# One maximum step of 11 units takes two key blocks in one, and attention's output is turned by DMA

## The chip, the cores and the metric

The kernel runs on one core of one Trainium2 chip. TensorE multiplies matrices into PSUM; VectorE, ScalarE and GpSimd (POOL in the profile) work on tiles; SP only issues DMAs and waits. The metric is the device time of one launch in microseconds. A time of the profile is that of one profiled execution.

## The reference

A transformer layer over 2048 rows of width 512, in bf16: layer norm, attention with 32 heads of width 16, a residual, layer norm, a gated feed-forward of width 1792, a residual.

```python
def _A_ref(x, wqkv, wo):
    B, S, D = x.shape
    H = 32
    Dh = D // H
    qkv = (lambda x, *d: x.transpose(*d))((x @ wqkv).reshape(B, S, 3, H, Dh), 2, 0, 3, 1, 4)
    q, k, v = qkv[0], qkv[1], qkv[2]
    scores = jnp.einsum("bhqd,bhkd->bhqk", q, k) * (Dh ** -0.5)
    p = _softmax(scores, axis=-1)
    o = jnp.einsum("bhqk,bhkd->bhqd", p, v)
    return (lambda x, *d: x.transpose(*d))(o, 0, 2, 1, 3).reshape(B, S, D) @ wo
...
h = x + _A_ref(_layernorm(x, axis=-1), A_wqkv, A_wo)
h2 = h + (_gelu(n @ w_gate) * (n @ w_up)) @ w_down        # n = _layernorm(h)
```

## The kernel before

**Units and ticks.** Attention is cut into 64 units: 8 groups of 256 query rows (`gi`), and in each 8 slots of four heads. A unit has 16 ticks. In each tick a *maximum pass* (`p1_pair`, `p1_consume`) has TensorE write two banks of scores, 128 queries x 512 keys for each of two heads (L797), and VectorE reduce both in one `tensor_reduce` of 1024 columns to two maxima in `PM` (L806). Tick j of a unit takes key block `j // 4`, query half `(j // 2) % 2`, and two of the four heads. GpSimd folds the four key blocks' maxima into the row maximum in steps (`negm_part` after ticks 8 and 12, L817 to L824; `negm_pre` after tick 15, L832 to L840), splits it into three bf16 terms, and SP turns them by a DMA transpose (`negm_post`, L846); four ticks later GpSimd adds the turned rows to the queries (L851), whose spare rows meet ones in the keys. So the scores come out of TensorE with their maximum subtracted.

**The second pass** follows 24 ticks behind (`P2_START`): in each tick TensorE computes two tiles of transposed scores of the earlier unit (`p2_tile`, L867: two matmuls of 256 columns into one bank), and ScalarE takes their exponentials (`p2_consume`, L896: 512 columns each). Banks 0 to 3 hold the maximum pass's two pairs; banks 4 to 7 are shared by the exponentials' tiles and one *dense* item at a time.

**The dense stream** (`Dense`) is everything else that TensorE does, cut into items that run a piece per tick: the products of the probabilities with the values (`item_pv`, L910, once in each unit), the turn of the output (`item_ofin`, L936), the output projection (`item_oproj`, L1015), and the feed-forward's gates, ups (L1089) and downs (L1139) of the group before. `prio` holds items with a due tick, `ready` the rest in order. A gate or an up starts only if the program's own count of ScalarE's backlog, `act_lag`, is at most `LAG_START`. Filler matmuls (L1299) take up what TensorE has left. `defer(k, fn)` runs a step k ticks later. `PoolStream` hands GpSimd its operations within a budget of 1.19 us a tick.

**Turn of the output.** After `item_pv`, ScalarE copies the 256 columns of a slot to `OA` (fp32). In every second unit `item_ofin` turns two slots with four fp32 matmuls against an identity, ScalarE copies the result to `OAT`, and GpSimd takes the inverse of the sums (a power, L945, 16 columns) and multiplies (L949) into `Otok`. When all eight slots of a group are there, `post_onT` turns `Otok` by DMA, and projection, residual, layer norm, `post_hnT` (a DMA transpose again) and the feed-forward of that group follow.

**Feed-forward.** A gate's item makes ScalarE copy the product to `g_sb`; GpSimd computes the polynomial (L1079, L1080, L1081), ScalarE the tanh (L1072), GpSimd two more steps (L1077, L1078) and, with the up's copy, the product (L1131). Seven pairs of gate and up and two downs make a group.

**The order of the work** on each engine is the order in which the program's loop over ticks emits it. Each engine runs its list in order, and each instruction waits for the semaphores of what it depends on. SP's list holds all DMAs.

**The tail.** After the last maximum, 24 ticks of exponentials are left, then the last group's projection, layer norm (its inverse root on GpSimd, L1262) and feed-forward (`tail_a`, `tail_b`); what of the dense stream is left then is run there.

Of the kernel before, what the change touches and what calls it, by code (L numbers as in the profile page):

```python
# [222 lines left out]
ADDX = 4  # L223
# [5 lines left out]
LAG_START = 0.4  # L229
LAG_OP = 0.2  # L230
TANH_LAG = 2


def bass_sequential_preLN__mha_block__geglu_ffn__prompt_kernel(nc, A_x, A_wqkv, A_wo, B_x, B_w_gate, B_w_up, B_w_down, out):
    dbg = None
    with ExitStack() as es:
# [74 lines left out]
        OAT = at("OAT", [128, 2, 272], FP32)  # L311
# [189 lines left out]
        def startable(it, room):  # L501
            if it[0] is item_gate and par_busy[it[1][1] % 2] and room < 10:
                return False
            if it[0] is item_down and it[1] == (GL - 1, 1) and not force[0]:
                return False
            if it[0] is item_down and it[1][1] == 0 and not force[0]:
                return not gut_left.get(it[1][0], 0) and dense.now >= gut_last.get(it[1][0], 0) + 1
            return it[0] is not item_projT or not (qks_busy.get(("a", qk_n[0] % 4)) or qks_busy.get(("b", qk_n[0] % 2)))

        class Dense:  # L510
            def __init__(self):
                self.prio = []
                self.ready = []
                self.gen = None
# [13 lines left out]
            def _start(self, item):  # L528
                genfn, a, est, nb = item
                if self.single:  # L530
# [5 lines left out]
            def piece(self):  # L536
                if self.single and self.pause > 0:
                    return 0
                while True:
                    if self.gen is None:  # L540
# [4 lines left out]
                        if self.prio and (not self.single or self.prio[0][3] <= self.now):  # L545
                            self._start(self.prio.pop(0))
                        elif self.ready and (not self.single or ((act_lag[0] <= LAG_START or force[0] or self.ready[0][0] not in (item_gate, item_up)) and startable(self.ready[0], lim - self.now) and self.ready[0][3] <= self.now and self.now + self.ready[0][2] + PAUSE - 1 <= lim)):
# [25 lines left out]
        dense = Dense()  # L573

# [19 lines left out]
        class PoolStream:  # L594

            def __init__(self):
                self.q = []
                self.budget = 0.0
            def add(self, ops, then=None):
# [4 lines left out]
            def spend(self, cost):  # L604
                self.budget -= cost
            def run(self, flush=False):
                while self.q and (flush or self.budget >= min(self.q[0][0], 1.0)):
                    if not flush and self.q[0][0] > 2.0 and dense.now % 16 in (1, 2, 3, 13, 14, 15):
                        break
                    cost, fn, then = self.q.pop(0)  # L610
                    self.budget -= cost
                    fn()
# [190 lines left out]
        def p1_consume(ui, tiles):  # L803
            par = ui % 2
            (b, qt, kc, g), (b2, _, _, g2) = tiles
            P.op("dve", lambda e: e.tensor_reduce(out=PM[:, par, qt, kc, g:g + 2], in_=pbank[:, b:b + 2, :], axis=AX.X, op=ALU.max),  # L806
                 reads=[("pb", b), ("pb", b2)], writes=[("PM", par, qt, kc, g), ("PM", par, qt, kc, g2)])

        def negm_part(ui, k):
# [10 lines left out]
            else:  # L820
# [3 lines left out]
                P.op("pool", lambda e: e.tensor_scalar(out=m3, in0=m3, scalar1=-1.0, scalar2=None, op0=ALU.mult), reads=[("MXm", par)], writes=[("MXm", par)])  # L824

# [16 lines left out]
        def negm_post(ui):  # L842
# [6 lines left out]
            def add():  # L849
                pool.spend(0.7)  # L850
                P.op("pool", lambda e: e.tensor_tensor(out=q_ap, in0=q_ap, in1=STG[:, par, :], op=ALU.add), reads=[("STG", par), ("qT", slot, c, hf)], writes=[("qT", slot, c, hf)])  # L851
                q_ready.add(ui)
            defer(ADDX, add)
# [45 lines left out]
        def item_pv(b, ui):  # L899
# [18 lines left out]
            evac_act(OA[:, par, 256 * col:256 * col + 256], pbank[:, b, 0:256], [("pb", b)], [("OA", par, col)], cost=0.41)  # L918
            if gi == GL and slot >= NSLOT - 2:
                if col == 0:  # L920
                    dense.add(item_ofin, gi, (slot,), front=True, est=3, not_before=dense.now + 3)
            elif col == 1:
                dense.add(item_ofin, gi, (slot - 1, slot), front=True, est=3, not_before=dense.now + 3)
# [6 lines left out]
        oat_busy = {}  # L930
        def item_ofin(b, gi, slots):
            gp, par, ns = gi % 2, slots[0] // 2 % 2, len(slots)
            assert not oat_busy.get(par), "GpSimd too far behind"
            for q in range(2):
                for sp in range(ns):
# [487 lines left out]
```

## Time and profile before

| | |
|---|---|
| median of 3 runs | 1243.8 us (1243.76 to 1245.08) |
| profiled execution | 1243.51 us |
| its span, first to last instruction | 1241.8 us |
| mean granted TensorE clock | 1.00 |
| VectorE busy | 1188.9 us, 1087 instructions |
| ScalarE busy | 1199.5 us, 2444 instructions |
| GpSimd busy | 764.4 us, 1540 instructions |

In the rows, `out<-in` names what an instruction writes and reads, then come partitions x elements and the type, `xcount`, the busy time in us, the mean duration in ns, and behind the second bar the idle time of the engine just before these instructions with what ended most of it. The durations of successive instructions of one engine overlap: the time that one more instruction costs is the distance from start to start, or a stretch's length over its count, not its duration. The chain of work that ended last is followed back from the last instruction to what released it. A row of a stretch has its bounds in us, its length, then the busy time and the count for PE, PEld, DVE, ACT and POOL (or for those that have any), the clock, the DMA engines' share and GB/s.

### The profile page before, as it was taken

The numbers are of one execution on the slowest core, as the hardware profiler recorded it, in microseconds if no ns is written. First come the engines' busy times: TensorE is split into PE (matmuls) and PEld (weight loads), VectorE is DVE, ScalarE is ACT, GpSimd is POOL, SyncE is SP. The second block draws the span as 40 slices with busy tenths as digits, with TensorE's granted clock in tenths as the row PEclk, the third lists the DMA queues.
The fourth block names the chain that finished last, engine by engine and source line by source line (L and its number), as shares of the span: only waits on it lengthen the run. The fifth ranks groups of instructions, "written<-read, shape, count | busy, mean of one in ns | idle before, by whom it ended". The sixth has DMA issues, their size and how long they took to land.

```text
span 1241.8 us, 31457 instructions
## 1 busy us (share of the span) xinstructions
PE 1137.1 (92%) x12700; PEld 438.6 (35%) x12700; DVE 1188.9 (96%) x1087; ACT 1199.5 (97%) x2444; POOL 764.4 (62%) x1540
## 2 busy tenths in 40 slices
PE   8999888899999999999999998999999999999989
PEld 3333222233333333333333333333333333333335
DVE  8999999999999999999999999999999999999933
ACT  7899999999999999999999999999999999999992
POOL 8557774467746765476645777367654767547760
PEclk9999999999999999999999999999999999999999
DMA  5101004300010000100010000100002000100000
GB/s 151 31 22 28 24 19 125 93 5 4 6 31 12 6 6 6 38 5 6 4 27 18 3 6 6 27 17 6 6 4 36 10 4 6 27 19 3 6 12 18
DMA packets 50800, 27.45 MB, mean 22 GB/s; under 512 B 36064, under 2 KB 49632, under 8 KB 50656
## 3 DMA queue, kind: packets, MB, share of 16 engines
q1 hardware_dynamic: 50656, 25.45, 8.3%
q8 instruction: 101, 1.65, 0.6%
q14 instruction: 43, 0.35, 0.1%
HBM read 11.80 MB, written 2.10 MB: 11 GB/s over the span
## 4 chain that ended last, share of the span: by engine, by line
DVE 60%; ACT 27%; PE 10%; POOL 2%; issue 1%; DMA 1%; POOLq 0%
DVE PM L806 60%; ACT PTM L896 14%; ACT PTG L896 4%; ACT PTE L896 3%; PE pbank L1139 2%; PE pbank L797 1%; PE pbank L867 1%; PE pbank L1089 1%; ACT th_sb L1072 1%; PE pbank L739 1%; ACT g_sb L641 1%; ACT OnT L1029 1%; PE pbank L427 1%; PE pbank L676 1%; DMA STG<-ST 1%
## 5 line engine op out<-in xcount | busy, mean ns | idle before, releaser
L806 DVE TENSOR_REDUCE PM<-pbank 128x2 f32<-128x1024 f32 x1024 | 1162.5, 1213 | 5.9 <-PE pbank L867 3.3
L896 ACT ACTIVATE PTM<-pbank 128x512 bf16<-128x512 f32 x1357 | 721.0, 668 | 4.7
L867 PE MATMUL pbank<-QT,KT 32*128 32x256 bf16 x4096 | 495.2, 273 | 12.2 <-ACT PTM L896 5.1
L797 PE MATMUL pbank<-KT,QT 32*128 32x512 bf16 x2048 | 394.2, 382 | 46.4 <-DVE PM L806 23.8
L1299 PE MATMUL pbank<-ones_bf,ident 128*128 128x512 bf16 x814 | 250.8, 384 | 27.3 <-ACT PTM L896 2.4
L797 PEld LDWEIGHTS pbank<-KT,QT 32*128 32x128 bf16 x2048 | 104.4, 91 | 392.5 <-DVE PM L806 170.3
L896 ACT ACTIVATE PTG<-pbank 128x512 bf16<-128x512 f32 x407 | 221.4, 660 | 0.8
L867 PEld LDWEIGHTS pbank<-QT,KT 32*128 32x128 bf16 x4096 | 163.6, 92 | 66.2 <-ACT PTM L896 34.7
L896 ACT ACTIVATE PTE<-pbank 128x512 bf16<-128x512 f32 x236 | 135.5, 668 | 0.8
L910 PE MATMUL pbank<-PTM,VA 128*17 128x256 bf16 x2776 | 125.7, 274 | 2.8 <-ACT PTM L884 0.9
L832 POOL TENSOR_TENSOR MX<-PM,MX 128x8 f32<-128x8 f32 x64 | 12.9, 202 | 163.6 <-DVE PM L806 163.6
L1299 PEld LDWEIGHTS pbank<-ones_bf,ident 128*128 128x128 bf16 x814 | 49.4, 97 | 132.5 <-ACT PTM L896 82.7
L945 POOL TENSOR_TENSOR LINV<-OAT,negone 128x16 f32<-128x16 f32 (+1 forms) x32 | 92.7, 2896 | 0.0
L910 PEld LDWEIGHTS pbank<-PTM,VA 128*17 128x17 bf16 x2776 | 59.8, 89 | 47.2 <-issue 29.8
L821 POOL TENSOR_TENSOR MX<-PM,MX 128x8 f32<-128x8 f32 x64 | 13.0, 203 | 101.6 <-DVE PM L806 101.5
L1089 PE MATMUL pbank<-hnT_l,wu_sb 128*128 128x256 bf16 x448 | 66.7, 275 | 3.1 <-ACT PTM L896 0.2
L1089 PE MATMUL pbank<-hnT_l,wg_sb 128*128 128x256 bf16 x448 | 66.9, 275 | 2.4
L1078 POOL TENSOR_TENSOR th_sb<-th_sb,g_sb 128x512 f32<-128x512 f32 x49 | 62.2, 1269 | 4.1
L1081 POOL TENSOR_TENSOR th_sb<-th_sb,g_sb 128x512 f32<-128x512 f32 x49 | 62.1, 1268 | 3.1
L1131 POOL TENSOR_TENSOR GUT<-th_sb,u_sb 128x512 bf16<-128x512 f32 x49 | 62.3, 1271 | 2.0
L1079 POOL TENSOR_TENSOR th_sb<-g_sb 128x512 f32<-128x512 f32 x49 | 51.0, 1041 | 19.2 <-ACT g_sb L641 19.2
L1139 PE MATMUL pbank<-wd_sb,GUT 128*128 128x512 bf16 x224 | 60.2, 382 | 0.6 <-ACT PTM L896 0.2
(154 smaller groups left out, 1100.0 us busy)
## 6 DMA issues: line engine op xcount, KB each, us to landing
QKS<-QKS SPq DMA_DIRECT2D x27, 112.0 KB, 2.2
x_sb<-in_A_x_dram SPq DMA_DIRECT2D x4, 512.0 KB, 5.7
xres<-in_A_x_dram SPq DMA_DIRECT2D x16, 128.0 KB, 2.2
out_dram<-out_sb SPq DMA_DIRECT2D x16, 128.0 KB, 1.9
wg_sb<-in_B_w_gate_dram SPq DMA_DIRECT2D x4, 448.0 KB, 5.2
wu_sb<-in_B_w_up_dram SPq DMA_DIRECT2D x4, 448.0 KB, 6.1
wd_sb<-in_B_w_down_dram SPq DMA_DIRECT2D x3, 512.0 KB, 5.5
STG<-ST SPq DMA_TRANSPOSE x64, 2.3
```

What stands on the lines that cost most here:

```text
L797: P.op("pe", lambda e, g=g, b=b: e.matmul(pbank[:, b, :], QT[32 * g:32 * g + 32, c, slot, 128 * qt:128 * qt + 128], KT[32 * g:32 * g + 32, ...
L806: P.op("dve", lambda e: e.tensor_reduce(out=PM[:, par, qt, kc, g:g + 2], in_=pbank[:, b:b + 2, :], axis=AX.X, op=ALU.max), reads=[("pb", b ...
L867: P.op("pe", lambda e, kt=kt, i=i: e.matmul(pbank[:, b, 256 * i:256 * i + 256], KT[32 * g:32 * g + 32, slot, 128 * kt:128 * kt + 128], QT[ ...
L896: P.op("act", lambda e, b=b, pi=pi: e.activation(out=PTt(pi), in_=pbank[:, b, :], func=ACT.Exp), reads=[("pb", b)], writes=[("PT", pi)], e ...
L910: P.op("pe", lambda e, g=g, kt=kt, pi=pi, i=i: e.matmul(pbank[32 * g:32 * g + 17, b, 0:256], VA[:, kt, 4 * slot + g, :], PTt(pi)[:, 256 * ...
L945: P.op("pool", lambda e: e.tensor_tensor(out=li, in0=oat4[:, :, :, 16], in1=negone[:, 0:8 * ns].rearrange("p (q h) -> p q h", q=2), op=ALU ...
L1078: o(1.27, lambda e: e.tensor_tensor(out=ts_, in0=ts_, in1=gs, op=ALU.mult), [("th", par), ("g", par)])], then=done)
L1081: o(1.27, lambda e: e.tensor_tensor(out=ts_, in0=ts_, in1=gs, op=ALU.mult), [("th", par), ("g", par)])], then=lambda: defer(TANH_LAG, lamb ...
L1089: P.op("pe", lambda e, dc=dc, fc=fc, i=i: e.matmul(pbank[:, b, 256 * i:256 * i + 256], w[:, dc, 128 * fc:128 * fc + 128], hT[:, dc, :], st ...
L1131: P.op("pool", lambda e: e.tensor_tensor(out=o_ap, in0=shp(ts_), in1=shp(us), op=ALU.mult), reads=[("th", par), ("u", par)], writes=o_keys ...
L1139: P.op("pe", lambda e: e.matmul(pbank[:, b, :], GUT[:, fc, 128 * k:128 * k + 128], wd_sb[:, fc, :], start=first, stop=last), reads=[("GUT" ...
L1299: P.op("pe", lambda e: e.matmul(pbank[:, b, :], ident[:], ones_bf[:, 0:512], start=True, stop=True), reads=["ident", "ones_bf"], writes=[( ...
```

## The change

In 11 of the 64 units the maximum over key blocks 2 and 3, for one query half and two heads, is taken in one step. TensorE computes the difference of the two blocks' scores (one matmul with the query, one with its negative `QN`, into one bank), ScalarE writes its positive part to `RB` in fp32, and VectorE adds that to block 2's scores and takes the maximum, max(a + relu(b - a)) = max(a, b), one `tensor_tensor_reduce` for each head. The reduction of block 3 (tick 14 of the unit) is left out: that tick is skipped in the loop, what was deferred moves by one tick, and the two exponential tiles of the skipped tick are taken one each in the next two odd ticks.

```diff
+JOINT = (12, 14, 17, 20, 25, 28, 33, 36, 41, 44, 49)
+J_AT, J_GONE = 10, 14
...
         def p1_consume(ui, tiles):
...
+            if ui in JOINT and (qt, kc, g) == (1, 2, 0):
+                assert y_left[ui] == 0, "differences too late"
+                for b_, g_ in ((b, g), (b2, g2)):
+                    P.op("dve", lambda e, b_=b_, g_=g_: e.tensor_tensor_reduce(out=RB[:, g_, :], in0=pbank[:, b_, :], in1=RB[:, g_, :], scale=1.0, scalar=-3.0e38, op0=ALU.add, op1=ALU.max, accum_out=PM[:, par, qt, kc, g_:g_ + 1]),
+                         reads=[("pb", b_), ("RB", g_)], writes=[("PM", par, qt, kc, g_), ("RB", g_)])
+                return
...
+        def joint_prep(ui):
+            gi, slot = units[ui]
+            c, qt = gi // 2, 2 * (gi % 2) + 1
+            y_left[ui] = 2
+            pool.add([(0.4, lambda: P.op("pool", lambda e: e.tensor_scalar(out=QN[:], in0=QT[:, c, slot, 128 * qt:128 * qt + 128], scalar1=-1.0, scalar2=None, op0=ALU.mult),
+                                         reads=[("qT", slot, c, gi % 2)], writes=["QN"]))], then=lambda: defer(1, lambda: dense.extra.extend([(item_diff, (ui, g), 2, 0) for g in (0, 1)])))
+
+        def item_diff(b, ui, g):
...
+            P.op("pe", lambda e: e.matmul(pbank[:, b, :], QT[32 * g:32 * g + 32, c, slot, 128 * qt:128 * qt + 128], KT[32 * g:32 * g + 32, slot, 1536:2048], start=True, stop=False, tile_position=(32 * g, 0)),
...
+            P.op("pe", lambda e: e.matmul(pbank[:, b, :], QN[32 * g:32 * g + 32, :], KT[32 * g:32 * g + 32, slot, 1024:1536], start=False, stop=True, tile_position=(32 * g, 0)),
...
+            act_more(0.48)
+            P.op("act", lambda e: e.activation(out=RB[:, g, :], in_=pbank[:, b, :], func=ACT.Relu), reads=[("pb", b)], writes=[("RB", g)], extra_deps=dG)
...
+            if p1_ok and tick // 16 in JOINT and tick % 16 == J_GONE:
+                for i, (k_, fn_) in enumerate(deferred):
+                    deferred[i] = (k_ + 1, fn_)
...
+                behind[0] += 2
+                tick += 1
+                dense.now = tick
+                continue
...
+            more = 1 if behind[0] and tick % 2 else 0
```

The difference's items stand in a third list of the dense stream, `extra`. While a unit of the 11 is at tick 12 or later, or tiles are still behind, `tight()` holds, and no gate, up or tanh starts; a down doesn't start there after tick 8:

```diff
+            if it[0] is item_down and not force[0] and (tight() or dense.now // 16 in JOINT and dense.now % 16 > J_GONE - 6 or act_lag[0] > LAG_START):
+                return False
...
+        def tight():
+            return dense.now // 16 in JOINT and dense.now % 16 >= J_GONE - 2 or bool(behind[0])
```

The output's turn: `item_pv` ends in a bf16 copy to `OB`, SP turns it by a DMA transpose, and GpSimd normalizes one slot at a time (an 8-column power, then the product). The last group's last two slots keep the way over TensorE.

```diff
+        def o_turn(ui):
...
+            P.dma("sp", lambda e: e.dma_start_transpose(out=OBT[:, par, :, :], in_=OB[:, par, :]), ("obT", par), reads=[("OB", par)], writes=[("OBT", par)])
+            o4 = OBT[:, par].rearrange("p q (g i) -> p q g i", i=32)
+            defer(5, lambda: o_norm(gi, slot, par, o4, ("OBT", par), ob_busy))
...
+            pool.add([(1.45, inv), (0.31, mul)], then=over)
...
+        def clear(fn):
+            if not force[0] and not 5 <= dense.now % 16 <= 14:
+                defer(1, lambda: clear(fn))
+            else:
+                fn()
```

`clear` keeps the DMA transposes of `post_onT` and `post_hnT` to ticks 5 to 14. The program counts GpSimd's time (`PoolStream.charge`, with `TICK` and `TOOK`), and a tanh is emitted only when by that count its polynomial is done (`poly_end`) and the backlog of ScalarE, with a running gate or up, is within `LAG_TH + SLOPE * n`. The inverse (`inv`) isn't handed to GpSimd in ticks 1 to 3 and 12 to 15 and may be at tick 0 whatever the budget. `negm_part` is called after ticks 9 and 13 and `negm_pre` with `negm_post` at the start of the next unit's first tick (`unit_end`); the add follows three ticks later (`ADDX = 3`). `LAG_START` goes from 0.4 to 0.3.

175 lines of the change are left out of this document (122 added, 53 removed).

## The prediction

> **What bounds the kernel now.** I read the engine totals first, then the chain of work that ended last, then the groups of instructions, and then single stretches.
>
> ```profile
> span 1241.8 us, 31457 instructions
> PE 1137.1 (92%) x12700; PEld 438.6 (35%) x12700; DVE 1188.9 (96%) x1087; ACT 1199.5 (97%) x2444; POOL 764.4 (62%) x1540
> DVE 60%; ACT 27%; PE 10%; POOL 2%; issue 1%; DMA 1%; POOLq 0%
> L806 DVE TENSOR_REDUCE PM<-pbank 128x2 f32<-128x1024 f32 x1024 | 1162.5, 1213 | 5.9 <-PE pbank L867 3.3
> L896 ACT ACTIVATE PTM<-pbank 128x512 bf16<-128x512 f32 x1357 | 721.0, 668 | 4.7
> 413.58 91.72 DVE PM L806 x81
> 551.50 1.96 ACT PTM L896 x4
> 341.20:486.90 145.70, 134.59 (x1550) 51.66 (x1548) 145.16 (x129) 144.75 (x301) 90.25 (x186) 1.00 0.05 12
> 1186.00:1242.00 56.00, 50.18 (x476) 28.39 (x476) 13.15 (x27) 32.31 (x43) 20.27 (x25) 1.00 0.05 16
> ```
>
> The maximum pass is 1024 reductions on VectorE (L806), and it was idle before them for 5.9 us in all. Their mean duration of 1213 ns overlaps the next one; the chain's row gives the true rate, 91.72 / 81 = 1.132 us each. 1024 x 1.132 = 1159 us of the 1241.8 us span. The last two rows (busy time of PE, PEld, DVE, ACT, POOL in a stretch) show eight units in 145.7 us, where 128 reductions at 1.132 us need 144.9, and the tail after the last reduction, 56 us, in which VectorE does almost nothing. So **VectorE sets the pace** until 1186 us, with ScalarE close behind, as a count of that stretch shows.
>
> By the program, a group of eight units gives ScalarE 256 exponentials, 27 others of 512 columns (7 gates, 7 ups, 7 tanh, and 2 each of projection, square and output), 12 short evacuations and four accumulator reads: 299, against the row's 301 with its cut edges. The chain's four exponentials in 1.96 us give 0.49 us each. The short ones:
>
> ```profile
> 1183.04 0.43 ACT L641 ACTIVATE OAT<-pbank 128x272 f32<-128x272 f32 x1
> 1183.32 1.62 ACT L896 ACTIVATE PTE<-pbank 128x512 bf16<-128x512 f32 x3
> ```
>
> From one start to the next is 0.28 us. So a group of eight units needs about 283 x 0.49 + 12 x 0.28 + 0.4 (an estimate for the four reads) = 142.4 us of ScalarE, 3.3 us less than it has: 2%. A gain on VectorE can be passed on only as far as ScalarE follows.
>
> **The change, part by part.**
>
> *Two reductions become two add-and-max instructions, 11 times.* In each of the 11 units one reduction (tick 14) goes, and the one at tick 10 is replaced by two tensor_tensor_reduce of 512 columns, one input in PSUM, one in SBUF. Removed: 22 x 1.132 = 24.9 us. The trace has no such instruction. The nearest rows:
>
> ```profile
> L1118 DVE TENSOR_TENSOR GUT<-pbank,th_sb 128x512 bf16<-128x512 f32 x7 | 4.8, 692 | 14.2 <-PE pbank L1089 14.2
> 1213.63 0.70 DVE L1253 BATCH_NORM_STATS2 stats<-pbank 128x6 f32<-128x512 f32 x1 [0.57 <-PE pbank L1250]
> 1214.25 0.68 DVE L1254 BATCH_NORM_STATS2 stats<-pbank 128x6 f32<-128x512 f32 x1
> 1214.85 0.30 DVE L1258 BATCH_NORM_AGGREGATE mv<-stats 128x2 f32<-128x6 f32 x2
> 1215.18 0.17 DVE L1261 TENSOR_SCALAR rstd<-mv 128x2 f32<-128x2 f32 x1
> ```
>
> A tensor_tensor on a PSUM and an SBUF operand of 512 columns lasts 0.692 us; two statistics of 0.70 and 0.68 us over as many PSUM columns start 0.62 and 0.60 us ahead of what follows. So 0.61 us is the lower end. The upper end is a separate tiny instruction that writes out the maximum: the two aggregations together take 1215.18 - 1214.85 = 0.33, 0.165 each, so 0.78. I take 0.66, nearer to the tensor_tensor row, since the reduction in the trace writes its result within its own time. Added: 22 x 0.66 = 14.5 us (13.4 to 17.2). Net -10.4 us (-11.5 to -7.7). Nothing hides it or covers it: this engine is the wall.
>
> The Trainium skill, page "VectorE: DVE Perf Modes", section "Two Vector instructions with no wait between them", says that an operation that also writes out its accumulator is two instructions, the main one and an accumulator read. No row here shows one on VectorE; by that rule the sum would take the upper end, 2.7 us later than with my value.
>
> *ScalarE's positive part and the difference on TensorE.* 22 Relu of 512 columns, each 0.49 us, are 10.8 us more on ScalarE, and 22 x 2 matmuls on TensorE stand where filler matmuls (L1299) run now: nothing there. Against that, 31 evacuations of the turned output (OAT) go, 31 x 0.28 = 8.7 us. A group with two such units then needs 142.4 + 4 x 0.49 - 4 x 0.28 = 143.2 us on ScalarE and has 145.7 - 2 x 0.94 = 143.8. It still fits, with 0.6 us instead of 3.3.
>
> *The exponentials of the tick that goes.* They are not dropped: two tiles follow, one more in each of the next two odd ticks. In the four ticks 13, 15, 16, 17 ScalarE has ten exponentials, 4.90 us, in 4 x 1.132 = 4.53 us; 0.37 us excess. TensorE issues the next maximum's matmuls behind exponentials' tiles that need a free bank, so an excess that the banks don't absorb reaches VectorE. What such a lateness looks like today:
>
> ```profile
> 339.12 30.78 DVE L806 TENSOR_REDUCE PM<-pbank 128x2 f32<-128x1024 f32 x27
> 370.19 5.75 DVE L806 TENSOR_REDUCE PM<-pbank 128x2 f32<-128x1024 f32 x5 [0.29 <-PE pbank L867]
> 376.12 9.14 DVE L806 TENSOR_REDUCE PM<-pbank 128x2 f32<-128x1024 f32 x8 [0.17 <-PE pbank L867]
> ```
>
> There VectorE idles 0.29 and 0.17 us in one unit where ScalarE has a projection's, an up's and an output's evacuations at once. Bounds per changed unit: 0, if the two or more tiles of lead in the four banks swallow 0.37 us, and 0.74, if it is felt in both of the longer ticks. I take 0.2: 11 x 0.2 = +2.2 us (0 to 8.1).
>
> *Output turned by DMA.* Fp32 transposes on TensorE (L936) and the evacuation from them go; 62 DMA transposes come, issued from SP behind ScalarE's evacuation of the same item.
>
> ```profile
> L846 SPq DMA_TRANSPOSE STG<-ST x64: 1168/1170/2163, 40.1 to 1188.1; - x64
> L936 PE MATMUL pbank<-ident,OA 128*128 128x128 f32 x126 | 27.6, 301 | 0.0
> L945 POOL TENSOR_TENSOR LINV<-OAT,negone 128x16 f32<-128x16 f32 x31 | 91.0, 2937 | 0.0
> L945 POOL TENSOR_TENSOR LINV<-OAT,negone 128x8 f32<-128x8 f32 x1 | 1.7, 1652 | 0.0
> ```
>
> Each costs SP 1.17 us in an issue queue with little else. The new transpose waits for an evacuation at about tick 9 of a unit; behind it on SP stands the maximum's transpose (L846) of tick 16, seven ticks (7.9 us) later, so it should find the queue free. GpSimd's inverses turn from 31 x 2.94 into 62 x 1.65 us, 91 to 102 us, on an engine 62% busy. A maximum's final add (L851) is no longer stuck behind 2.9 us in one piece. Cost taken: 0 (a gain of up to 1.2 us at the end of the pass, where the last 16-wide inverse lies in the chain; a loss only if GpSimd or SP becomes late for the eight ticks between a unit's maximum and its use).
>
> *GpSimd's time counted in the program, and later starts.* These only order the stream of gates, ups, downs and tanh; no work is added. They can remove some of today's lateness on VectorE (145.7 - 144.9 = 0.8 us per eight units, some 6 to 7 us in all) or push feed-forward work later. I take 0 for both and keep them as rivals.
>
> **The sum:** 1243.5 (the profiled execution; span 1241.8) - 24.9 + 14.5 + 2.2 = **1235.3 us**. The median of the runs is 1243.8, 0.3 us higher, so nothing needs correcting.
>
> **The rivals.**
>
> *More gain.* The excess of 0.37 us stays within the banks and half of today's lateness goes: 1235.3 - 2.2 - 3.5 = 1229.6. For it: today's lateness comes at the same place in each group, where ScalarE gets several evacuations at once, and the change tests ScalarE's backlog before more of them. Against it: ScalarE has less to spare.
>
> *ScalarE takes over.* Each changed unit passes its excess on twice, 0.74 us: 1235.3 + 11 x 0.54 = 1241.2. For it: 0.6 us of room per group. Against it: VectorE idled only 5.9 us before its reductions in a kernel whose ScalarE has 2% of room.
>
> *The change doesn't save VectorE's time.* Where each new instruction takes 1.1 us instead of 0.66, whether from the SBUF operand against GpSimd or from its own program, 22 x 1.13 = 24.9 and the gain is nil: 1243.5 + 2.2 = 1245.7. GpSimd's fp32 instructions (1.27 us) are the nearest of that size. The Trainium skill, page "SBUF — State Buffer", section "SBUF: two separate sides", has VectorE and GpSimd exclude each other when VectorE reads two SBUF inputs or runs in a mode with two ports; here one input lies in PSUM, so by it there is no such wait. No run here shows it yet.
>
> *Slower: feed-forward work is left for the tail.* No gate or up starts from tick 12 of a changed unit until the two tiles are caught up, and no down from tick 9.
>
> ```profile
> 384.80:402.90 18.10, 3.63 (x25) 1.82 (x26) 1.00 0.03 5
> 402.90:421.10 18.20, 3.04 (x20) 1.53 (x20) 1.00 0.03 6
> L1078 POOL TENSOR_TENSOR th_sb<-th_sb,g_sb 128x512 f32<-128x512 f32 x49 | 62.2, 1269 | 4.1
> L1081 POOL TENSOR_TENSOR th_sb<-th_sb,g_sb 128x512 f32<-128x512 f32 x49 | 62.1, 1268 | 3.1
> L1131 POOL TENSOR_TENSOR GUT<-th_sb,u_sb 128x512 bf16<-128x512 f32 x49 | 62.3, 1271 | 2.0
> L1079 POOL TENSOR_TENSOR th_sb<-g_sb 128x512 f32<-128x512 f32 x49 | 51.0, 1041 | 19.2 <-ACT g_sb L641 19.2
> L1080 POOL TENSOR_SCALAR th_sb<-th_sb 128x512 f32<-128x512 f32 x49 | 30.4, 621 | 4.3
> POOL rstd L1262 <- DVE rstd L1261: 8.7, 1, 8.7
> ```
>
> The first two rows are gate and up matmuls (L1089) in two successive units: 25 and 20, two to three items of eight a unit. A group has 14, and two downs take most of a unit each, so five and a half units of gates and two of downs fill nearly all eight today. A changed unit loses one or two items; the removed turn of the output gives one back in every second unit. If that doesn't balance over units 12 to 49 and the 14 unchanged units behind them don't make it up, gate-and-up pairs run in the tail. Each costs GpSimd 3 x 1.27 + 1.04 + 2 x 0.62 = 6.1 us in one chain; the tail hides 8.7 us of that, GpSimd's wait before the last layer norm's inverse root (L1262). Three pairs too many: 18.3 - 8.7 = 9.6 us, 1235.3 + 9.6 = 1244.9; four: 1251. It decides from (8.2 + 8.7) / 6.1 = 2.8 pairs. Against it: the 14 last units have room of 14/8 x (3.3 + 1.1) = 7.7 us on ScalarE, about five pairs at 3 x 0.49.
>
> **How the numbers follow.** Forecast (1232 to 1240) 0.52; more gain 0.14; ScalarE takes over 0.13; no saving on VectorE 0.06; work left for the tail 0.15. A measurement of this kernel tells a change from none at about 0.2%, 2.5 us. Faster by more than that: 0.52 + 0.14 + 0.07 of the takeover = 0.73. Within: the takeover's other 0.06 and half of no saving, 0.03, = 0.09. Slower: 0.15 + 0.03 = 0.18. The range 1229 to 1245 takes in all of the forecast, its bounds (-11.5 and 0; -7.7 and +8.1 falls at 1243.9), most of the greater gain and the takeover, and leaves out the dearer half of the tail's cases and the odd end of the others: about 0.15.
>
> **What would show it.** A reduction count of 1002 and 22 add-and-max rows on VectorE, each about 0.74 us long and 0.66 apart; the last of them some 8 us before 1186 in the new span; VectorE's idle time a few us larger, at ticks 15 to 18 of the 11 units; a tail of still about 56 us, with the same feed-forward items in it. I am wrong if the new rows are a microsecond long, if VectorE's idle time grows by 8 us or more, or if the tail grows by more than 3.

## The result, and the profile after

The changed kernel takes **1239.9 us** (median of six runs, 1238.9 to 1240.7) against 1243.8 (1243.6 to 1245.1): a ratio of 0.9968 [0.9958, 0.9978], 3.9 us less. The forecast was 1235.3, 8.2 us less than its base. The profiled execution took 1240.23 us. One launch of all those below, of the kernel with one joint step a group, took 4515.45 us at full clock and is left out of its median.

From the page of the kernel after: the span, the engines' totals, the chain that ended last by engine, and the group of the reductions (busy time and mean ns, behind the second bar the idle time before them):

```profile
span 1238.5 us, 31200 instructions
PE 1099.2 (89%) x12389; PEld 429.3 (35%) x12588; DVE 1182.2 (95%) x1111; ACT 1196.3 (97%) x2433; POOL 785.3 (63%) x1624
ACT 59%; DVE 30%; PE 8%; issue 1%; POOL 1%; DMA 1%
L840 DVE TENSOR_REDUCE PM<-pbank 128x2 f32<-128x1024 f32 x1002 | 1141.9, 1213 | 11.3 <-PE pbank L904 7.4
```

The chain has turned over. Before, VectorE held 60% of it and ScalarE 27%; now ScalarE holds 59% and VectorE 30%. VectorE idles 11.3 us before its reductions where it was 5.9, mostly until a tile of the second pass (L904, formerly L867) has come out of TensorE. Before these tiles TensorE itself waits most for exponentials (6.5 us in 22 waits for L933), which still read the bank.

The new instructions, in the groups of the kernel after and in its timeline (start, duration):

```profile
L837 DVE CUSTOM_DVE_ANT_0 OA<-pbank,OA 128x512 f32<-128x512 f32 x22 | 14.2, 683 | 0.0
L837 DVE DVE_READ_ACCUMULATOR2_ANT PM<- 128x1 f32 x22 | 1.8, 83 | 0.0
L1027 ACT ACTIVATE OA<-pbank 128x512 f32<-128x512 f32 x22 | 16.5, 748 | 0.0
```

```profile
249.32 0.68 DVE L837 CUSTOM_DVE_ANT_0 OA<-pbank,OA 128x512 f32<-128x512 f32 x1
249.93 0.08 DVE L837 DVE_READ_ACCUMULATOR2_ANT PM<- 128x1 f32 x1
249.93 0.69 DVE L837 CUSTOM_DVE_ANT_0 OA<-pbank,OA 128x512 f32<-128x512 f32 x1
250.54 0.08 DVE L837 DVE_READ_ACCUMULATOR2_ANT PM<- 128x1 f32 x1
250.54 3.48 DVE L840 TENSOR_REDUCE PM<-pbank 128x2 f32<-128x1024 f32 x3
```

(`RB` shows under the name `OA`.) A joint step takes 250.54 - 249.32 = 1.22 us in place of two reductions, 2 x 1.132: 1.045 us saved, 11.5 us in all 11.

How much of that arrived is read from where the last maximum ends. Three timelines of VectorE have its last stretch of reductions; the first is of before, the second of after, the third of the changed kernel without joint steps (first experiment):

```profile
1174.58 11.39 DVE L806 TENSOR_REDUCE PM<-pbank 128x2 f32<-128x1024 f32 x10
```

```profile
1173.89 9.19 DVE L840 TENSOR_REDUCE PM<-pbank 128x2 f32<-128x1024 f32 x8
```

```profile
1174.83 11.55 DVE L840 TENSOR_REDUCE PM<-pbank 128x2 f32<-128x1024 f32 x10
```

Start and length give 1185.97, 1183.08 and 1186.38. With the span, the tail behind it is 55.8, 55.4 and 52.2 us. So after against before: the pass ends 2.9 us sooner where VectorE's work shrank by 11.5, and the tail is shorter by 0.4. So 11.5 - 2.9 = **8.6 us were lost inside the pass**; that is what the experiments look for.

### The profile page after: what moved, and what is told of

Its sections match the earlier page's. It is cut to its first block, busy times and chain, and to the rows that moved or that the text cites. A ratio compares the mean times of both kernels' runs of the same rounds, so it can differ in the third digit from the quotient of the medians.

```text
span 1238.5 us, 31200 instructions
## 1 busy us (share of the span) xinstructions
PE 1099.2 (89%) x12389; PEld 429.3 (35%) x12588; DVE 1182.2 (95%) x1111; ACT 1196.3 (97%) x2433; POOL 785.3 (63%) x1624
## 4 chain that ended last, share of the span: by engine, by line
ACT 59%; DVE 30%; PE 8%; issue 1%; POOL 1%; DMA 1%
ACT PTM L933 33%; DVE PM L840 29%; ACT PTG L933 10%; ACT PTE L933 6%; PE pbank L1220 2%; ACT th_sb L1148 2%; ACT u_sb L669 2%; ACT g_sb L669 1%; PE pbank L825 1%; ACT PTM L921 1%; PE pbank L904 1%; PE pbank L1380 1%; PE pbank L1168 1%; ACT OB L669 1%; ACT OnT L1101 1%
## 5 line engine op out<-in xcount | busy, mean ns | idle before, releaser
L840 DVE TENSOR_REDUCE PM<-pbank 128x2 f32<-128x1024 f32 x1002 | 1141.9, 1213 | 11.3 <-PE pbank L904 7.4
L933 ACT ACTIVATE PTM<-pbank 128x512 bf16<-128x512 f32 x1357 | 727.4, 704 | 6.6 <-PE pbank L904 2.0
L904 PE MATMUL pbank<-QT,KT 32*128 32x256 bf16 x4096 | 517.6, 273 | 17.8 <-ACT PTM L933 6.5
L825 PE MATMUL pbank<-KT,QT 32*128 32x512 bf16 x2026 | 390.5, 384 | 25.3 <-DVE PM L840 10.7
L1380 PE MATMUL pbank<-ones_bf,ident 128*128 128x512 bf16 x639 | 206.0, 384 | 65.0 <-ACT PTM L933 31.9
L933 ACT ACTIVATE PTG<-pbank 128x512 bf16<-128x512 f32 x407 | 227.6, 704 | 1.2
L825 PEld LDWEIGHTS pbank<-KT,QT 32*128 32x128 bf16 x2026 | 98.7, 91 | 367.6 <-DVE PM L840 134.4
L904 PEld LDWEIGHTS pbank<-QT,KT 32*128 32x128 bf16 x4096 | 171.5, 92 | 90.4 <-ACT PTM L933 47.2
L933 ACT ACTIVATE PTE<-pbank 128x512 bf16<-128x512 f32 x236 | 137.3, 700 | 0.6
L981 POOL TENSOR_TENSOR LINV<-OBT,negone 128x8 f32<-128x8 bf16 x62 | 103.4, 1667 | 0.0
L1168 PE MATMUL pbank<-hnT_l,wg_sb 128*128 128x256 bf16 x448 | 66.6, 274 | 2.8 <-ACT PTG L933 0.2
L1168 PE MATMUL pbank<-hnT_l,wu_sb 128*128 128x256 bf16 x448 | 66.5, 275 | 2.8 <-ACT PTM L933 0.2
L888 POOL TENSOR_TENSOR QT<-QT,STG 128x256 bf16<-128x256 bf16 x64 | 42.7, 668 | 35.0 <-DMA STG<-ST 35.0
```

What stands on the lines that cost most here:

```text
L825: P.op("pe", lambda e, g=g, b=b: e.matmul(pbank[:, b, :], QT[32 * g:32 * g + 32, c, slot, 128 * qt:128 * qt + 128], KT[32 * g:32 * g + 32, ...
L904: P.op("pe", lambda e, kt=kt, i=i: e.matmul(pbank[:, b, 256 * i:256 * i + 256], KT[32 * g:32 * g + 32, slot, 128 * kt:128 * kt + 128], QT[ ...
L933: P.op("act", lambda e, b=b, pi=pi: e.activation(out=PTt(pi), in_=pbank[:, b, :], func=ACT.Exp), reads=[("pb", b)], writes=[("PT", pi)], e ...
L981: P.op("pool", lambda e: e.tensor_tensor(out=li, in0=o4[:, :, :, 16], in1=negone[:, 0:8].rearrange("p (q h) -> p q h", q=2), op=ALU.pow), ...
L1168: P.op("pe", lambda e, dc=dc, fc=fc, i=i: e.matmul(pbank[:, b, 256 * i:256 * i + 256], w[:, dc, 128 * fc:128 * fc + 128], hT[:, dc, :], st ...
L1380: P.op("pe", lambda e: e.matmul(pbank[:, b, :], ident[:], ones_bf[:, 0:512], start=True, stop=True), reads=["ident", "ones_bf"], writes=[( ...
```

## The experiments

Theories for the loss: *ScalarE is full*, so that each joint step's two positive parts, 2 x 0.49 us, come back as waits of VectorE; the rival, which the prediction had, is that only *the two ticks behind the skipped one* are too full; a second rival is *TensorE*, stalled on DMAs or at a lower clock; a third is that the *dense stream* loses places, and pays in the tail.

All results together; each ratio is to the kernel before, run beside it on the same chip. "Last max" is the end of the last maximum and "tail" the span less that, in the profiled execution; "idle" is the listed idle time before reductions; us.

| kernel | median | ratio to before | last max | tail | idle |
|---|---|---|---|---|---|
| before | 1243.8 | | 1186.0 | 55.8 | 5.9 |
| after | 1239.9 | 0.9968 [0.9958, 0.9978] | 1183.1 | 55.4 | 11.3 |
| no joint step | 1239.7 | 0.9971 [0.9961, 0.9981] | 1186.4 | 52.2 | 5.2 |
| positive part of 2 columns | 1236.9 | 0.9945 [0.9930, 0.9961] | 1181.1 | 55.4 | 10.7 |
| exponentials of 448 | 1225.9 | 0.9860 [0.9846, 0.9873] | 1169.4 | 55.4 | 3.0 |
| third tile short | 1238.7 | 0.9966 [0.9954, 0.9978] | 1183.3 | 55.4 | 12.0 |
| projection 2 ticks later | 1246.8 | 1.0023 [1.0014, 1.0033] | 1180.7 | 63.7 | 8.4 |
| 10 joint steps, moved | 1238.1 | 0.9953 [0.9940, 0.9965] | 1183.9 | 52.2 | 8.5 |
| 13 joint steps | 1240.5 | 0.9971 [0.9961, 0.9982] | 1183.0 | 55.4 | 9.8 |
| more filler | 1292.1 | 1.0389 [1.0375, 1.0403] | 1235.1 | 55.4 | 32.2 |
| one joint step a group | 1236.9 | 0.9945 [0.9932, 0.9959] | 1184.0 | 52.2 | 7.5 |
| positive part twice | 1260.7 | 1.0137 [1.0110, 1.0165] | 1206.2 | 55.4 | 31.3 |
| exponentials of 504 | 1234.0 | 0.9920 [0.9905, 0.9935] | 1178.3 | 55.4 | 9.6 |
| one a group, feed-forward later | 1238.4 | 0.9958 [0.9945, 0.9972] | 1180.5 | 55.0 | 5.4 |
| an item in the turn's place | 1256.9 | 1.0108 [1.0095, 1.0122] | 1184.6 | 70.3 | 5.4 |

### Without the joint steps

```diff
-JOINT = (12, 14, 17, 20, 25, 28, 33, 36, 41, 44, 49)
+JOINT = ()
```

> The changed kernel without any joint step: 1024 reductions as before, the output's turn by DMA and the new starting rules stay. Theory A (ScalarE is overcommitted over stretches of two to three units, because 22 positive parts came in and VectorE's time shrank under it): ScalarE loses 8.7 us of evacuations, so VectorE's idle time before its reductions is at or under the 5.9 us of the kernel before; the time is 1242 to 1243.5 us. Theory B (the lateness comes from the turn by DMA and the new order on SP, GpSimd and TensorE): VectorE's idle time stays at about 11 us and the time is 1247 to 1249 us. Neither my own first step (a peak of ScalarE in the two catch-up ticks) nor A expects TensorE's clock to fall in the middle.

Measured: the same time as the whole change, 0.9971 [0.9961, 0.9981]. VectorE's idle time is 5.2 us, as theory A has it, but 1239.7 us lies below what either theory expected: neither saw that this part gains. So the joint steps bring nothing here, and **the output's turn by DMA with the new start rules brings the whole gain**; which of these two does was not separated. The two get there differently. Their tails, in windows of one line each: first before, gates and ups (L1089) in the whole tail and downs (L1139) behind the last exponential, then the same for after (L1168, L1220), then for this kernel:

```profile
1186.00:1241.80 55.80, 16.18 (x136) 13.06 (x136) 1.00 0.05 16
1210.10:1241.80 31.70, 13.55 (x56) 5.44 (x56) 1.00 0.05 18
```

```profile
1183.10:1238.50 55.40, 18.29 (x152) 14.46 (x152) 1.00 0.06 17
1206.90:1238.50 31.60, 13.13 (x54) 5.44 (x56) 1.00 0.05 18
```

```profile
1186.40:1238.60 52.20, 14.08 (x120) 11.59 (x120) 1.00 0.06 18
1209.40:1238.60 29.20, 10.20 (x42) 4.06 (x42) 1.00 0.05 15
```

A down is 14 matmuls, a gate or an up 8, and the last group's 14 gates and ups (112) always lie in the tail. Without joint steps 8 gate and up matmuls of the group before are left instead of 24, and 42 matmuls of downs (three downs) instead of 56 (four) behind the exponentials: the earlier group's down fits under the exponentials, and TensorE has 13.55 - 10.20 = 3.3 us less to do where nothing hides it. The stretch behind the exponentials is 2.5 us shorter (29.2 for 31.7); the other 1.1 of the tail's 3.6 us lie among the exponentials, where two gates or ups fewer stand. With the joint steps 40 matmuls are left and the down is back (54 are recorded; the weight loads beside them are 56). So the joint steps earn 1186.4 - 1183.1 = 3.3 us in the pass and lose 55.4 - 52.2 = 3.2 in the tail.

### ScalarE's work made smaller and larger

Five kernels change only columns or counts of ScalarE's instructions (in the first, `RB` is also cleared once at the start; `w` holds once each buffer for the probabilities has been written whole). Four of them leave out part of the result.

```diff
-out=RB[:, g, :], in_=pbank[:, b, :], func=ACT.Relu
+out=RB[:, g, 0:2], in_=pbank[:, b, 0:2], func=ACT.Relu
```

> The positive part is taken of 2 of 512 columns (the rest of RB keeps old values: this leaves out block 3 in the joint maxima). Order, waits and the program's own counts are the same; ScalarE has 22 x 0.43 = 9.4 us less. Theory A: the lateness of VectorE's reductions, 16.7 us in the changed kernel, shrinks by some 3 us; 1236 to 1238 us. Theory B: unchanged, 1239 to 1240.5 us. Peak in the catch-up ticks: unchanged, since the positive parts lie elsewhere.

```diff
-out=PTt(pi), in_=pbank[:, b, :], func=ACT.Exp
+out=PTt(pi)[:, 0:w], in_=pbank[:, b, 0:w], func=ACT.Exp      # w = 448
```

> Exponentials of 448 of 512 columns from the second time round their buffers (the last 64 columns keep old values: part of the softmax is left out). Same order; ScalarE has about 0.053 us less in each of some 1900, 1.7 us a unit, and is nowhere near its limit. Theory A: nearly all of VectorE's lateness goes, in the joint units, before and behind them: lateness 2 to 4 us and the last maximum at about 1171 us; the time near 1225 us (the end of the pass also shortens its tail by about 2 us). Theory B: lateness stays at 10 us or more, the last maximum at 1178 us or later.

```diff
-                p2_consume(ui_, [t])
+                p2_consume(ui_, [t], 128 if n_ == 2 else 512)      # the third tile of a tick
```

> Only the 22 exponentials that are taken as a third one in a tick, to catch up, cover 128 of 512 columns (part of the softmax is left out). ScalarE has 22 x 0.32 = 7 us less, all in the catch-up ticks. Peak in the catch-up ticks (the prediction's step): all that was added goes, lateness falls to about 8 us, 1232 to 1235 us. Theory A: those ticks count only as part of the stretch, so lateness falls by about 2.5 us; 1237 to 1238 us. Theory B: unchanged.

Measured: the last maximum comes 2.0, 13.7 and -0.3 us sooner than after. The third figure hides a gain, for in that profiled execution the clock was halved for 5 x 3.4 us inside the pass, after has 2 x 3.4. In units 24 to 31, where neither has any (fourth and second of the windows below), the group takes 144.46 us against 145.21: 0.75 us sooner for 4 x 0.32 = 1.3 us less of ScalarE. **The rival that the two ticks hold the whole loss is out**: its 1232 to 1235 us didn't come in any of five runs (1237.4 to 1240.6). Those ticks count, but as part of ScalarE's work. Of the 11.5 us saved on VectorE, all arrives once ScalarE is busy for 6% less (135.57 us for 144.60): the last maximum is 16.6 us ahead of before, these 11.5 and 5 of the lateness of before. The profile's chain of that kernel, by engine, and its group of reductions:

```profile
DVE 88%; PE 6%; ACT 5%; DMA 1%; POOL 1%; issue 0%; POOLq 0%
L840 DVE TENSOR_REDUCE PM<-pbank 128x2 f32<-128x1024 f32 x1002 | 1136.0, 1211 | 3.0 <-PE pbank L825 1.7
```

VectorE is the wall again, 88% of the chain. One group of eight units (24 to 31, with two joint steps), in windows with the busy time of PE, PEld, DVE, ACT and POOL; before, after, without joint steps, third tile short, and with 448 columns:

```profile
456.65:602.38 145.73, 134.60 (x1550) 51.54 (x1548) 145.19 (x129) 144.75 (x300) 90.23 (x186) 1.00 0.06 12
```

```profile
452.97:598.18 145.21, 131.41 (x1509) 50.97 (x1533) 143.82 (x134) 144.60 (x301) 93.35 (x198) 1.00 0.08 16
```

```profile
455.88:601.42 145.54, 133.27 (x1541) 49.54 (x1542) 145.39 (x129) 144.33 (x296) 91.89 (x195) 1.00 0.07 16
```

```profile
455.48:599.94 144.46, 135.78 (x1533) 51.11 (x1532) 143.47 (x133) 143.68 (x301) 93.33 (x198) 1.00 0.09 16
```

```profile
451.96:594.68 142.72, 125.49 (x1532) 46.74 (x1532) 142.72 (x134) 135.57 (x300) 93.30 (x198) 1.00 0.08 16
```

Two joint steps should take 2.1 us off a group. They take off 145.54 - 145.21 = 0.3. ScalarE is busy for 144.60 of 145.21 us there; with 448 columns it has 7 us to spare, VectorE is busy for all of 142.72, and the group is 2.5 us shorter. Not every group lost so much. These are the two groups before this one, which also have two joint steps each; after, then without joint steps:

```profile
164.97:308.64 143.67, 123.69 (x1466) 44.28 (x1490) 143.13 (x134) 142.17 (x289) 81.13 (x182) 1.00 0.20 56
308.64:452.89 144.25, 128.66 (x1498) 49.16 (x1521) 143.65 (x133) 143.36 (x297) 84.26 (x189) 1.00 0.08 16
```

```profile
165.15:310.26 145.11, 129.03 (x1517) 46.34 (x1516) 145.10 (x130) 143.49 (x292) 95.61 (x193) 1.00 0.20 56
310.26:455.80 145.54, 134.32 (x1548) 51.00 (x1548) 145.38 (x130) 144.75 (x299) 97.85 (x201) 1.00 0.07 16
```

There 1.4 and 1.3 of the 2.1 us arrive; ScalarE has 1.5 and 0.9 us free in them, where in units 24 to 31 it has 0.6. Two more points of the dose:

```diff
+out=PTt(pi)[:, 0:w], in_=pbank[:, b, 0:w], func=ACT.Exp      # w = 504
```

> Exponentials of 504 of 512 columns (the last 8 keep old values: a little of the softmax is left out); ScalarE has about 0.0067 us less in each, 1.7 us in a group of eight units. Theory D: a group with two joint steps falls from 145.2 to about 143.6 us, near VectorE's own 142.7; the last maximum at 1174 to 1176 us, tail 55.4; 1231 to 1233 us. Narrow form of A: half of that, 1235 to 1237 us. Theory B: unchanged.

```diff
+            P.op("act", lambda e: e.activation(out=RB[:, g, :], in_=pbank[:, b, :], func=ACT.Relu), reads=[("pb", b)], writes=[("RB", g)], extra_deps=dG)      # a second time
```

> The changed kernel with each positive part taken twice, the same result written again: 22 x 0.49 = 10.8 us more for ScalarE, order and counts as before. Theory D (a joint step trades 1.05 us of VectorE for 0.98 us of ScalarE, and in units 16 to 51 ScalarE is the one that ends last, with some 2.2 us in eight units that it can't use): a group of eight units with two joint steps grows by 4 x 0.49 = 2.0 us, from 145.2 to 147.2, and the last maximum comes 8 to 10 us later; 1247 to 1250 us. If only single crowded spots of ScalarE count (theory A in its narrow form), a few us: 1242 to 1245 us. Theory B (TensorE, DMA): unchanged, 1239 to 1240.5.

The same group with 504 columns:

```profile
453.44:597.55 144.11, 135.16 (x1533) 50.59 (x1532) 143.39 (x133) 143.34 (x300) 93.66 (x198) 1.00 0.08 16
```

ScalarE is busy for 1.3 us less, the group is 1.1 us shorter, and the last maximum comes 4.8 us sooner; theory D had 7 to 9, and the time lies between its range and that of A's narrow form. With 22 more positive parts, 22 x 0.49 = 10.8 us, it comes 23.1 us later, and the idle time before reductions is 31.3 us instead of 11.3. That is more than ScalarE's added work and than any theory expected. In that execution the clock was 0.982 on the mean against 0.997. The four runs of this kernel go from 1256.2 us at a clock of 0.992 to 1265.5 at 0.981, 0.85 us for each thousandth; carried on to 0.997 (an estimate) that is 1252 us, 12 over after, near the 10.8 added. So the rest goes with the lower clock; why more work on ScalarE lowers it isn't shown. Down and up, **the end of the pass follows ScalarE**, which was the question, but not at a fixed rate.

### Stalls of TensorE and its clock

Two stretches of the profile after stand out. Rows of its timeline at 1085 us, and windows (busy PE, PEld, DVE, ACT, POOL, then the granted clock):

```profile
1085.17 3.38 SPq L1067 DMA_TRANSPOSE OnT<-Otok  x2
1088.53 0.60 PE L1087 MATMUL pbank<-wo_sb,OnT 128*128 128x512 bf16 x2 [1.75 <-DMA OnT<-Otok]
1089.49 2.53 DVE L840 TENSOR_REDUCE PM<-pbank 128x2 f32<-128x1024 f32 x2 [1.07 <-PE pbank L904]
```

```profile
1086.60:1090.10 3.50, 1.75 (x17) 0.45 (x11) 2.43 (x3) 2.19 (x6) 2.61 (x6) 1.00 0.38 78
1090.10:1093.50 3.40, 3.40 (x18) 0.74 (x17) 2.99 (x3) 3.16 (x8) 2.24 (x8) 0.50 0.01 2
816.90:820.40 3.50, 2.84 (x22) 0.79 (x20) 3.30 (x4) 3.50 (x9) 3.04 (x9) 1.00 0.00 0
820.40:823.80 3.40, 3.07 (x31) 0.82 (x30) 2.51 (x3) 2.87 (x7) 2.34 (x7) 0.51 0.09 19
```

In the first, the projection (L1087) is first in TensorE's list while its turned input is still under way; the maximum pass behind it in the same list waits too, and VectorE idles 1.07 us. In the next 3.4 us the clock is half, and VectorE loses 0.41 more. At 820.4 the clock halves without such a wait, and VectorE loses 0.89 of 3.40. Together that is up to 2.4 us of the 5.4 by which the listed idle time grew. It shows in the last eight units, which have no joint step, before and after:

```profile
1040.16:1185.97 145.81, 134.13 (x1544) 51.19 (x1542) 145.27 (x129) 144.83 (x301) 90.30 (x186) 1.00 0.06 13
1034.66:1183.08 148.42, 130.97 (x1526) 52.04 (x1548) 145.92 (x129) 146.02 (x302) 103.85 (x207) 0.99 0.07 16
```

They take 2.6 us longer, the stall and the half clock of unit 58 among them. In before the granted clock is full from end to end of the span, and TensorE waits for no such DMA.

```diff
-            dense.add(item_oproj, gi, k, front=True, est=3, not_before=dense.now + 4)
+            dense.add(item_oproj, gi, k, front=True, est=3, not_before=dense.now + 6)
```

> The changed kernel with the output projection started six ticks behind its DMA transpose instead of four. In the changed kernel TensorE stood 2.0 us on that transpose in unit 58, ScalarE and VectorE behind it, and its clock was halved for 3.4 us just after. If the stall is what cost VectorE 2.2 us there, the time falls by about 2 us, to 1237.5 to 1238.5 us, and no fall of the clock is left in unit 58. If VectorE was late there for ScalarE's sake, it stays at 1239 to 1240.5 us.

```diff
-                want = 2
+                want = 3      # fillers in a tick
```

> The changed kernel with one filler matmul more in each tick that has room (three units of TensorE work a tick instead of two). If too little TensorE work in some windows halves the clock, each time for 3.4 us at about 1 us of lateness, the falls go but for the one behind the stall in unit 58, and the time falls by about 1 us, to 1238.5 to 1239.5 us. If TensorE itself is short of time, lateness grows by several us: 1242 us or more.

Projections two ticks later: no wait on that DMA, no half clock in unit 58, and the last maximum 2.4 us sooner, as expected; and yet 1246.8 us instead of 1237.5 to 1238.5, for the tail grew by 8.3. Gates and ups in the tail of this kernel:

```profile
1180.70:1244.30 63.60, 19.31 (x160) 15.29 (x160) 0.97 0.05 14
```

The feed-forward hangs on the projection; 160 - 112 = 48 matmuls of the group before are left, 40 in after. Of them 16 run behind the last exponential, where after has none, and the clock is halved there for 3.4 us. More filler kept the clock at full speed throughout, but TensorE became the bound (72% of the chain) and 52 us were lost against after. What makes the clock halve stays open.

### Other places for the joint steps

```diff
+JOINT = (16, 18, 24, 26, 32, 34, 40, 42, 48, 50)
```

> Joint steps in 10 other units: 16, 18, 24, 26, 32, 34, 40, 42, 48, 50, that is at the start and two units behind the start of a group instead of one and four behind it, everything else as changed. Theory A (it is the placing: ScalarE is overcommitted in the units around the group's projection, and the joint units of the change lie before and behind these): VectorE saves 10 x 1.05 = 10.5 us and loses some 3 us more than without joint steps; the last maximum is at 1179 to 1181 us, and one down less is left for the tail, which is 52 us as without joint steps; 1232 to 1235 us. Rival C (any joint step is paid back by ScalarE, wherever it stands): as with none, 1239 to 1241 us.

```diff
+JOINT = (10, 16, 18, 24, 26, 32, 34, 40, 42, 48, 50, 52, 54)
```

> The same with three units more: 10, 52 and 54. Theory A: 3 x 1.05 us more off VectorE and about 1 us more lateness, but more feed-forward work left at the end, so a tail of 55 us again: 1233 to 1236 us, no better than ten. Rival C: 1239 to 1241 us.

```diff
+JOINT = (15, 23, 31, 39, 47, 55)
```

> One joint step in a group: units 15, 23, 31, 39, 47, 55. By theory D ScalarE and VectorE balance at about one a group: without any, a group takes 145.55 us, of which ScalarE works 141.1 and can't use 2.2, so 2.25 us are left, and each joint step takes 1.05 + 0.98 = 2.03 of them. So each of the six gains about 1 us over no joint step, with the short tail of 52 us: 1233 to 1235.5 us, the fastest yet. If every joint step is paid back wherever it stands: as with ten moved ones or none, 1237.5 to 1240 us.

Ten at other places keep the short tail (52.2) and 2.5 us of the pass: 1238.1 us, between what theory A and rival C expected. Thirteen fall back to the long tail, and to rival C's time. **Six, one in each of six groups, give the fastest version that computes the whole layer**: four runs of 1235.8 to 1238.0 us, 0.9945 [0.9932, 0.9959], 2.4 us better in the last maximum than none, with the same 52.2 us of tail. Its interval overlaps that of the ten, and 2.4 us is less than half of the 6 that theory D expected. Part of what it still loses are waits of TensorE on the transposed input of the feed-forward (waits, with total us, times and longest):

```profile
PE pbank L1168 <- DMA hnT_l<-OnT: 3.8, 4, 2.2
```

```diff
-                defer(3, lambda: add_ffn_when(gi))
+                defer(5, lambda: add_ffn_when(gi))      # six joint steps
```

> One joint step in a group as before, and the feed-forward of a group released five ticks after its last DMA transpose is emitted instead of three. With one joint step TensorE stood 3.8 us in all on that transpose (2.2 us in unit 35, where VectorE was 1.5 us late at once). If that is the reason why six joint steps gave only part of their 6.3 us, the last maximum comes 1.5 to 2.5 us earlier, at about 1182 us; 1234.5 to 1236.5 us. If ScalarE pays the joint steps back anyway, the lateness only moves: 1237 to 1239 us.

The same row of this kernel, and its downs behind the last exponential:

```profile
PE pbank L1168 <- DMA hnT_l<-OnT: 0.2, 1, 0.2
```

```profile
1203.80:1235.40 31.60, 13.07 (x53) 5.44 (x56) 1.00 0.05 18
```

The waits go and the last maximum comes 3.5 us sooner, more than expected. But 56 matmuls of downs (53 recorded; 56 weight loads) are behind the exponentials again, where with six joint steps and the old delay it was 42, the tail is 55.0, and the time isn't better than with the old delay: 0.9958 [0.9945, 0.9972].

### Putting the turn's place back

Without joint steps, an empty item of two fillers, one a tick, takes up the dense stream where the old turn stood.

```diff
+            if slot % 2 == 1 and not (gi == GL and slot >= NSLOT - 2):
+                dense.add(item_block, front=True, est=3, not_before=dense.now + 3)
...
+        def item_block(b):
+            dummy(b, 1)
+            yield 1
+            dummy(b, 1)
+            return 1
```

> The changed kernel without joint steps, with an item of two filler matmuls in the dense stream in every second unit, at the place and with the due tick that the output's turn over TensorE had; it does nothing else. Theory E (without joint steps the turn by DMA gains because the dense stream has room again, so that one down of 14 matmuls, 3.3 us, is done ahead of the tail): the tail is 55 to 56 us again and the time 1242.5 to 1246 us. Rival (it gains by ScalarE's missing evacuations or by the new starting rules): the tail stays at 52 us, and the time at 1239 to 1240.5 us.

Gates and ups in its tail (L1176 there), and its idle before reductions:

```profile
1184.60:1254.90 70.30, 22.41 (x176) 16.93 (x176) 0.93 0.04 13
```

```profile
L840 DVE TENSOR_REDUCE PM<-pbank 128x2 f32<-128x1024 f32 x1024 | 1161.6, 1211 | 5.4 <-PE pbank L904 2.1
```

The pass itself isn't slower (1184.6). The whole loss, 17 us, lies in the tail, 70.3 us against 52.2: 176 - 120 = 56 gate and up matmuls more are left there, the down is back, and the granted clock is 0.93 on the mean. Theory E had the direction, but a tail of 55 to 56 us. So a place in the dense stream is worth microseconds, though the item gives ScalarE nothing and TensorE only two fillers. That the loss is far larger than the old turn's, whose tail was 55.8 us, presumably comes from the new start rules, which stand beside the item here; it isn't shown. What the rules alone do was not tried, nor were the joint steps with the old turn.

## Why the prediction was wrong in its size

By the measured terms the profiled execution is 1243.5 - 11.5 (VectorE) + 8.6 (lost in the pass) - 0.4 (tail) = 1240.2, where the 8.6 is what is left over and not a cost measured by itself. Against the forecast VectorE gave 1.1 us more, the tail 0.4, and the pass lost 8.6 instead of 2.2. Step by step:

**VectorE's saving: right, at the favourable bound.** I took 10.4 of 7.7 to 11.5; it is 11.5. The upper end was a separate instruction that writes out the maximum. There is one, as the Trainium skill, page "VectorE: DVE Perf Modes", section "Two Vector instructions with no wait between them", says: 83 ns. But it starts together with the next main instruction and adds nothing from start to start; the sum by that rule, 2.7 us later, didn't come about. So the rival of no saving is out as well.

**"It still fits, with 0.6 us instead of 3.3": this is the step that failed.** I counted ScalarE's instructions by distances between starts and believed the rest to be room. The stretch's own row, quoted right there, has ScalarE busy for 144.75 of 145.70 us (and VectorE for 145.16). The row was the better guide: by my count a group with two joint steps needs 143.2 us, and units 24 to 31 took 145.2, so 2.0 us of the counted room stayed unused. What holds it back was not measured by itself. A joint step trades 1.04 us of VectorE for 0.98 of ScalarE; where both are nearly full, little of that is gained: 0.3 of 2.1 us in these units, 1.4 and 1.3 in the two groups before them.

**The excess of the ticks behind the skipped one (+2.2, bounds 0 to 8.1): wrong in place and in size.** 8.6 us came, above the upper bound, and not in those ticks alone (third tile short: 0.75 us of the 1.8 that units 24 to 31 lost). It is ScalarE over the whole group, and for up to 2.4 us a late DMA and half-clock stretches of TensorE, of which the prediction had nothing. The rival "ScalarE takes over" (1241.2, chance 0.13) had the right engine and nearly the right time, by the wrong ticks.

**Output turned by DMA, cost 0: wrong.** I priced its instructions on SP, GpSimd and ScalarE, which indeed cost next to nothing (without joint steps the pass ends 0.4 us later than before), and left out what its place in the dense stream is worth: by itself, with the start rules, it shortens the tail by 3.6 us and the time to 0.9971 of before. I had even written that "the removed turn of the output gives one back in every second unit", but as a set-off in a rival, not as a gain.

**Later starts, cost 0: wrong by as much the other way.** With the joint steps in place, 152 - 120 = 32 gate and up matmuls more than without stay for the tail and the down with them, 3.2 us. My rival "left for the tail" named the direction, but priced GpSimd's chain at 6.1 us a pair behind a cover of 8.7; what it cost was one down on TensorE, 3.3 us, without a cover. The tail "of still about 56 us" held (55.4) by luck: two errors of over 3 us cancelled.

**VectorE's idle time** rose by 5.4 us, below the 8 that I had named as the mark of being wrong, while 8.6 us were lost: listed idle time isn't all of the lateness, and the end of the last maximum is the safer mark.

## What to carry to other kernels

When two engines are both busy for 99% of a stretch by its own row, moving work from one to the other gains a part at best until the second is relieved; here 2.0 us of the "room" counted from start distances went unused in a group. Before costing a moved or removed step at nothing, count the places it holds in every ordered list, and read what would then fit: here a removed item that cost no engine anything was worth, with the new start rules, a whole down in the tail, and delays of the dense stream came back there. Price the parts of a change one by one, the main one above all: here the part beside it made the gain.

## What the runs showed of the hardware

The accumulator's read-out on VectorE lasts 83 ns and is free from start to start. One add-and-max over 512 columns of PSUM and SBUF takes 0.61 us from start to start; two take 1.22 where one reduction of 1024 PSUM columns takes 1.132.

TensorE's clock was halved for 3.4 us at a time in the middle of a run, once behind a wait of 1.75 us and once with TensorE busy for 2.84 of the 3.50 us ahead. The Trainium skill, page "TensorE: Matmul & The Clock Gate", section "Part 1: The HAM clock gate (the "warmup" mystery)", has the half clock come after an idle window of about 3.4 us. The length agrees; the idle window doesn't, for none of that length stands ahead of either. By the trace's clock records each stretch lasts 3.413 us or twice that, and those of one execution begin a whole multiple of 3.413 apart: 79 times in after, 48, 85 and 121 times with the third tile short. The clock goes with part of the scatter of the changed kernel's runs: spans of 1237.2 twice at a mean clock of 1.000, of 1237.7 and 1238.7 at 0.999, of 1238.5 and 1238.9 at 0.997.
